# A FNet and SwiGLU block on one core: five of the second products by Strassen's seven products in place of eight

## The chip, the core and the metric

The kernel runs on one core of a Trainium2 chip. The engines named below are PE (TensorE, the matmuls), DVE (VectorE), ACT (ScalarE), POOL (GpSimd, which here issues the adding DMAs) and SP (SyncE, which issues the other DMAs). The metric is the device time of one execution in microseconds (us); a shorter time is better.

## The reference

An adaptive layer norm and a Fourier mixing layer come first (sequence 2048, width 512), then a second adaptive layer norm gives `h`, and then the gated feed-forward block, which is where the change is:

```python
gate = jnp.einsum("bsd,df->bsf", x, w1)      # 2048 x 512 times 512 x 1792
up   = jnp.einsum("bsd,df->bsf", x, w3)
h    = _silu(gate) * up                      # 2048 x 1792
out  = jnp.einsum("bsf,fd->bsd", h, w2)      # 2048 x 1792 times 1792 x 512
...
x = x + gb * out                             # gb: one factor for each of the 512 columns
```

All data are float32.

## The kernel before

**Tiles.** Everything is held transposed: 128 features on the partitions, 512 sequence positions (one of four chunks t = 0 to 3) in the free dimension. The 1792 inner features are cut into seven groups g of 256. The chunks are worked on in pairs: the first pair is chunks 0 and 2, the second pair chunks 1 and 3. A step i of the last loop is one group of one pair: steps 0 to 4 are groups 2 to 6 of the first pair, steps 5 to 11 are groups 0 to 6 of the second pair.

**Precision.** A float32 product is made of three matmuls (`PASSES`, line 42): each operand is split into a rounded high part and the low rest, and high x high, high x low and low x high are added in one PSUM bank. The high part is a copy by ACT (`copy`, L87), the low part a subtraction by DVE (`minus`, L90). So every operand that TensorE multiplies costs one instruction on ACT and one on DVE.

**Units.** TensorE's work in this part comes in units of six matmuls of 128x512. The first products of a step (with w1, called a, and with w3, called b) are already done by the Strassen-Winograd scheme in seven units a1 to a7 and b1 to b7 (`factor`, from line 1239), in which several units add into one PSUM bank after another, with a read of the bank by ACT or DVE between. The second products of a step (with w2, called y) are eight plain units, one for each chunk of the pair and each 128 output columns (`down_unit`, line 1115): two halves of the group, three matmuls each. ACT reads the bank, scales it by gb (`copy_by`, L335) into half of a tile `y`, and after every second unit POOL issues a DMA that adds the tile onto `sums` in device memory (L1146). The last two groups of the second pair don't use `sums`: DVE adds their products onto `xr`, which `load_sums` has read back (L1106), and SP stores it.

**Order.** A written list sets the order of the units: `body` and `head` near line 1660 hold, for each step, its own units, the last three b units of the step before ("-b7 -b4 -b3"), and a "y" wherever the next unit of the second products of the step before is taken from the queue `seconds`. Everything else hangs on the units. `behind(n, fn)` holds a piece of ACT or DVE work back by n units. `jobs` is a queue of the splitting of the weights (and their Strassen sums): after each unit `beside` lets as many of them go as a budget of DVE and ACT time for that unit allows; `drain` makes those that a unit needs go at once. Tiles come from a pool of 50 slots, first freed first taken, so a tile may have to wait for whatever last read its slot, an adding DMA too. All engines run their own instructions in order.

Of the kernel before, what the change touches and what calls it, by code (L numbers as in the profile page):

```python
# [8 lines left out]
F32 = mybir.dt.float32  # L9
# [6 lines left out]
P = 128  # L16
# [26 lines left out]
def folded(nc, pools, c, cp, wmr, wmc, x, xt, ctr, cti, wdr, wdi, w1, w3, w2, out):  # L43
# [22 lines left out]
    def give(t):  # L66
        slot, _ = slot_of.pop(id(t))
        free.append(slot)
# [26 lines left out]
    def times(dst, a, b):  # L95
        nc.vector.tensor_tensor(out=dst, in0=a, in1=b, op=OP.mult)  # L96
# [1018 lines left out]
    def down_unit(g, pair, t, d, key):  # L1115
        last = g == NG - 1

        own = pair == 1 and g >= NG - 2
        if not own and d % 2 == 0:
            ys[0] = take(F32, "y")  # L1120

        parts = 2 if own and last and (t, d) == (NT - 1, ND - 1) else 1
        for n in range(parts):
            at = slice(n * N // parts, (n + 1) * N // parts)
            to = bank(down_banks[0] + turn[1] % down_banks[1])[:, at]
            turn[1] += 1
            for q in range(2):
                product(
                    to,
                    [u[:, q, cols(d)] for u in wuse[key]],  # L1130
                    [hf[g, t, q][:, b, at] for b in range(2)],
                    q == 0,
                    q == 1,
                )
            if own:
                xs = xr[t][d // 2][:, d % 2, at]
                nc.vector.scalar_tensor_tensor(
                    xs, to, gb[:, d : d + 1], xs, op0=OP.mult, op1=OP.add
                )
                if last:  # L1140
                    nc.sync.dma_start(out[t, d, :, at], xs)
            else:
                copy_by(ys[0][:, d % 2, :], to, gb[:, d : d + 1])
        if not own and d % 2 == 1:
            y = ys.pop(0)
            nc.gpsimd.dma_start(sums[t, d // 2], y, accum_op=OP.add)  # L1146
            behind(4, lambda: give(y))
            if last:
                behind(8, lambda i=d // 2: store(t, i))
        if d == ND - 1:  # L1150
            for q in range(2):
# [56 lines left out]
    TO = {1: 0, 6: 0, 7: 0, 4: 0, 2: 1, 5: 2, 3: 2}  # L1208
    state, vs = {}, {}

    def right(pair, n):
        t0, t1 = PAIRS[pair]
        if n in (1, 2, 3):
            at = {1: (t0, 0), 2: (t0, 1), 3: (t1, 1)}[n]
            return h2h[at], h2l[at]
        at = pair, {5: 1, 6: 2, 7: 3, 4: 4}[n]
        return th[at], tl[at]

    def result(i, w, q, k, src):

        g, pair = items[i]
        v = vs[i][q][:, k, :]
        if w == "w1":
            behind(k != 0 or q == 0, lambda: nc.scalar.activation(v, src, AF.Silu))  # L1224
            return
        times(v, v, src)

        def highs():
# [8 lines left out]
        behind(2, lows)  # L1237

    def factor(i, w, n):
# [18 lines left out]
        if n == 1:  # L1258
            st["x"] = take(F32, "x")
            if w == "w1":  # L1260
                vs[i] = [take(F32, "v") for _ in range(2)]
        if n == 5:
            st["y"] = take(F32, "x")
        if n in (1, 5, 6):
            copy(st["y" if n == 5 else "x"][:, n // 6, :], to)
        elif n == 4:
            result(i, w, 1, 0, to)
        else:

            own = st["y" if n == 7 else "x"][:, n % 2 if n < 7 else 0, :]  # L1270
            q, k = {2: (0, 0), 3: (0, 1), 7: (1, 1)}[n]
            dst = vs[i][q][:, k, :] if w == "w1" else own
            plus(dst, to, own)
            result(i, w, q, k, dst)
            if n == 7:
                behind(1, lambda: give(st["y"]))
        if n == 3:
            for x in wuse.pop(key).values():
                give(x)
            behind(1, lambda: give(st["x"]))  # L1280
            if w == "w3":
                for x in vs.pop(i):
                    behind(3, lambda x=x: give(x))


    loads.extend((n, m) for n in range(len(steps)) for m in range(2))
# [289 lines left out]
                up_block(g, t, q, w)  # L1576
                beside(2.72, USED[w])

    def down(g, pair, t, d, key):
        drain(lambda: (key, "l") in done, jobs)  # L1580
        delayed()
        down_unit(g, pair, t, d, key)
        beside(1.36, USED["own" if pair == 1 and g >= NG - 2 else "y"])

    for w in ("w1", "w3"):
# [25 lines left out]
    def other_operands():  # L1611
# [6 lines left out]
                give(h.pop((0, n)))  # L1618
        sum_parts(jobs, *sums_of.pop())

    def unit(kind, i, n):
# [12 lines left out]
        if (kind, n) == ("a", 1) and more:  # L1634
            load_w(("w1", *items[i + 1]))
        if (kind, n) == ("a", 6):
            load_w(("w2", g, pair))
        if (kind, n) == ("a", 3) and more:
            load_w(("w3", *items[i + 1]))
            weight_jobs(i + 1, "w1")  # L1640
        if (kind, n) == ("b", 2):
            plain_jobs(("w2", g, pair))
        if (kind, n) == ("b", 3):
            if i + 2 == turning:
                drain(lambda: ("xc", 3) in done)
# [5 lines left out]
            if more:  # L1651
                weight_jobs(i + 1, "w3")
            for t in PAIRS[pair]:
                seconds.extend((g, pair, t, d, ("w2", g, pair)) for d in range(ND))
        beside(1.36, FACTOR[kind][n])

    weight_jobs(0, "w3")
# [1 line left out]
    ln2(3)  # L1659
    for i in range(len(items)):  # L1660
        body = "a6 a5 y a7 y y a4 y a3 y b1 y b2 y b6 b5 y"
        if i == turning:
            body = "y y y y y a6 y a5 y a7 y b1 b2 a4 b6 a3 b5"
        if i == len(items) - 1:
            body = "a6 a5 y a7 y y a4 y a3 b1 y b2 b6 b5 y b7 y b4 y b3 y y y y y y y y"
        head = "-b7 a1 -b4 -b3 a2 " if i == turning else "-b7 a1 a2 -b4 -b3 " if i else "a1 a2 "
        for at in (head + body).split():
            if at == "y":
                if (i, len(seconds)) == (len(items) - 1, 4):
                    tc.mark_branch_hint_location("general", hint="LikelyTaken")  # L1670
# [809 lines left out]
```

## Time and profile before

| | |
|---|---|
| median of three runs | 711.03 us (710.54 to 712.84) |
| the profiled execution | 708.46 us, its span 706.7 us |
| PE busy | 686.3 us, 97% of the span |
| DVE busy | 548.3 us, 78% |
| ACT busy | 430.8 us, 61% |
| POOL busy | 119.4 us, 17% |
| chain that ended last | PE 81%, DVE 7%, ACT 6% |

The chain is followed back from the last instruction: at each step to what released it, or to the instruction before it on its engine. A matmul's row in the trace is longer (0.39 us) than the distance to the next one, because matmuls overlap; the distance is what counts. The steps 6 to 11, which the change touches, run from about 501 us to the end.

### The profile page before, as it was taken

Reading aid. Unit: us, or ns where it says so; the run is one execution under the profiler, and the core shown is the slowest. Engines: PE = TensorE matmul, PEld = TensorE weight load, DVE = VectorE, ACT = ScalarE, POOL = GpSimd, SP = SyncE. Lnnn points to the kernel's source line nnn. Section 1 sums busy time; section 2 is a strip of 40 time slices with the busy share of each in tenths; the row PEclk is TensorE's granted clock in tenths of the full one; section 3 lists DMA queues with packets and bytes.
Section 4 is the critical chain, followed back from the end, with each engine's and each line's share of the span. In section 5 each row is a group of like instructions: output and inputs, shape, how many; then the busy total and the mean of one; then the engine's idle time right before and its main releaser. Section 6 shows DMA issues by size and latency. Waiting matters only on the chain.

```text
span 706.7 us, 8912 instructions
## 1 busy us (share of the span) xinstructions
PE 686.3 (97%) x3152; PEld 564.7 (80%) x3152; DVE 548.3 (78%) x877; ACT 430.8 (61%) x709; POOL 119.4 (17%) x141
## 2 busy tenths in 40 slices
PE   7999999999999999899999999999999999999995
PEld 4898888888888888687888788787788888888784
DVE  5999679997999978579987886896865556664763
ACT  4998865545454655745677676867665565656420
POOL 1320253542524000200100101011010100101000
PEclk9999999999999999999999999999999999999998
DMA  8730299796678521522868558376763847537403
GB/s 266 211 120 1 77 373 328 251 307 229 207 283 287 168 86 41 92 58 64 209 114 199 89 130 153 61 156 137 239 136 73 180 62 175 111 69 162 137 0 124
DMA packets 38100, 108.93 MB, mean 154 GB/s; under 512 B 4896, under 2 KB 5152, under 8 KB 38048
## 3 DMA queue, kind: packets, MB, share of 16 engines
q0 software_dynamic: 12352, 43.00, 29.3%
q1 hardware_dynamic: 25264, 63.98, 27.5%
q10 hardware_dynamic: 432, 1.31, 0.5%
q8 instruction: 26, 0.43, 0.3%
q14 instruction: 26, 0.21, 0.1%
HBM read 76.81 MB, written 33.55 MB: 156 GB/s over the span
## 4 chain that ended last, share of the span: by engine, by line
PE 81%; DVE 7%; ACT 6%; issue 2%; DMA 2%; SPq 1%; ACTq 0%; DVEq 0%
PE bank L100 52%; PE bank L750 25%; PE bank L559 2%; PE bank L598 1%; DMA wmr<-in_wmr 1%; ACT xc L894 1%; PE bank L576 1%; DVE xc L96 1%; SPq L231 1%; ACT hf L87 1%; ACT y L335 1%; DVE v L96 0%; DVE hl L90 0%; ACT hm L501 0%; DMA w<-in_wdi 0%
## 5 line engine op out<-in xcount | busy, mean ns | idle before, releaser
L100 PE MATMUL bank<-hf,w2h 128*128 128x512 f32 (+1 forms) x452 | 140.9, 391 | 0.3
L1146 POOL DMA_DIRECT2D sum<-y x48 | 41.0, 855 | 390.1 <-ACT y L335 373.0
L100 PEld LDWEIGHTS bank<-hf,w2h 128*128 128x128 f32 x452 | 84.3, 188 | 22.1 <-DVE hf L90 3.4
L100 PE MATMUL bank<-hf,w2l 128*128 128x512 f32 (+1 forms) x226 | 87.6, 388 | 0.0
L87 ACT ACTIVATE hf<-v 128x512 fp32r<-128x512 f32 x56 | 35.3, 630 | 67.3 <-DVE v L96 62.7
L335 ACT ACTIVATE y<-bank,gb 128x512 f32<-128x512 f32 x96 | 64.9, 682 | 18.6 <-PE bank L100 18.3
L93 DVE TENSOR_TENSOR v<-bank,x 128x512 f32<-128x512 f32 x36 | 24.7, 685 | 34.9 <-PE bank L100 34.8
L750 PE MATMUL bank<-bh,us 128*128 128x512 f32 x128 | 49.9, 390 | 0.0
L93 DVE TENSOR_TENSOR x<-bank,x 128x512 f32<-128x512 f32 x36 | 24.7, 687 | 32.4 <-PE bank L100 28.7
L750 PE MATMUL bank<-bh,ul 128*128 128x512 f32 x128 | 49.8, 389 | 0.0
L750 PE MATMUL bank<-d,us 128*128 128x512 f32 x128 | 49.8, 389 | 0.0
L750 PE MATMUL bank<-d,uh 128*128 128x512 f32 x128 | 49.8, 389 | 0.0
L750 PE MATMUL bank<-l,us 128*128 128x512 f32 x128 | 49.8, 389 | 0.0
L750 PE MATMUL bank<-l,uh 128*128 128x512 f32 x128 | 49.8, 389 | 0.0
L100 PEld LDWEIGHTS bank<-hf,w2l 128*128 128x128 f32 x226 | 42.4, 188 | 8.4
L90 DVE TENSOR_TENSOR hf<-v,hf 128x512 fp32r<-128x512 f32 x56 | 38.5, 687 | 12.2 <-ACT hf L87 12.1
L170 POOL DMA_INDIRECT re<-in_ctr,mirror x32 | 35.8, 1117 | 66.2 <-DVE ul L90 39.5
L1224 ACT ACTIVATE v<-v 128x512 f32<-128x512 f32 x36 | 22.8, 632 | 38.8 <-DVE v L93 38.8
L87 ACT ACTIVATE x<-bank 128x512 f32<-128x512 f32 x72 | 41.4, 586 | 7.2 <-PE bank L100 6.5
L170 POOL DMA_INDIRECT im<-in_cti,mirror x32 | 32.7, 1023 | 35.3 <-PE bank L750 10.0
L100 PE MATMUL bank<-h2h,w1h 128*128 128x512 f32 x80 | 31.8, 397 | 1.5 <-ACT h2h L87 1.5
L100 PE MATMUL bank<-h2l,w1h 128*128 128x512 f32 x80 | 31.9, 399 | 0.8 <-DVE h2l L90 0.8
(246 smaller groups left out, 1775.2 us busy)
## 6 DMA issues: line engine op xcount, KB each, us to landing
sum<-y POOLq DMA_DIRECT2D x48, 512.0 KB, 5.6
w<-in_w SPq DMA_DIRECT2D x42, 512.0 KB, 4.5
re<-in_ctr SPq DMA_DIRECT2D x32, 256.0 KB, 5.0
im<-in_cti SPq DMA_DIRECT2D x32, 256.0 KB, 5.0
wmc<-in_wmc SPq DMA_DIRECT2D x8, 512.0 KB, 6.3
xr<-in_xt SPq DMA_DIRECT2D x8, 512.0 KB, 7.6
sum<-xr SPq DMA_DIRECT2D x8, 512.0 KB, 6.2
x<-in_x SPq DMA_DIRECT2D x11, 256.0 KB, 4.8
```

What stands on the lines that cost most here:

```text
L87: nc.scalar.activation(dst, src, AF.Copy, scale=scale)
L90: nc.vector.tensor_tensor(out=dst, in0=a, in1=b, op=OP.subtract)
L93: nc.vector.tensor_tensor(out=dst, in0=a, in1=b, op=OP.add)
L96: nc.vector.tensor_tensor(out=dst, in0=a, in1=b, op=OP.mult)
L100: nc.tensor.matmul(acc, lhs[a], rhs[b], start=first and n == 0, stop=last and n == len(PASSES) - 1, skip_group_check=more,)
L170: nc.gpsimd.indirect_dma_start(dst, None, rows, bass.IndirectOffsetOnAxis(ap=at, axis=0))
L231: queue.dma_start(raw_w[dt][q * 64 : (q + 1) * 64, m, :], w[i][par::2, q])
L335: nc.scalar.activation(dst, src, AF.Identity, scale=by)
L559: nc.tensor.matmul(halves(hb[k])[:, m, :], sides((hh, hl)[a][k])[:, dt, m, :], wu[dt][:, b, m, :], start=False, stop=dt % 2 == 1 and n == ...
L750: nc.tensor.matmul(acc[what, e], lhs, rhs, start=begin and i == 0, stop=(end or (turn and what == "x")) and i == len(terms) - 1, skip_grou ...
L1146: nc.gpsimd.dma_start(sums[t, d // 2], y, accum_op=OP.add)
L1224: behind(k != 0 or q == 0, lambda: nc.scalar.activation(v, src, AF.Silu))
```

## The change

For groups 0 to 4 of the second pair (steps 5 to 9) the second products are done by seven products instead of eight units. A product of this kind is also six matmuls: three into bank 6 and three into bank 7, for one chunk-sized right operand. Three of the seven start new sums in the two banks and four add onto what is there, and after each of them ACT copies both banks, scaled by gb, to a tile y that POOL adds onto `sums`. The right operands are four quarters of the gated product and three sums of them; the weights w2 get sums and a split of the sums, as w1 and w3 have. The order of the units is written anew for steps 6 to 11, with a seven-product unit after every two units of first products. The splitting of w3 for the next step is queued earlier (after b6 instead of after b3), and in step 5 that of w1 after a7 instead of a3. `load_sums` of both chunks now follows the seventh product of group 4, in step 11.

```diff
+    SEVEN = [(g, 1) for g in range(NG - 2)]
+    ORDER7 = (2, 5, 3, 1, 6, 7, 4)
+    LEFT7 = {1: "h0", 2: "h2", 4: "h3", 5: "s0", 6: "s1", 7: "s2", 3: "s3"}
+    TO7 = {2: (0, 0), 5: (1, 1), 3: (0, 1), 1: (0, 0), 6: (0, 1), 7: (1, 1), 4: (1, 0)}
...
+    def seven_parts(i, q, k):
...
+        if (q, k) != (0, 1):
+            n = {(0, 0): 1, (1, 0): 2, (1, 1): 3}[q, k]
+            behind(1, lambda: high(n, v[q, k]))
+            behind(2, lambda: low(n, v[q, k]))
+            return
+        t1, t2, t3, t4 = v[0, 0], v[1, 1], v[0, 1], v[1, 0]
+        behind(1, lambda: minus(t1, v[0, 1], v[0, 0]))
+        behind(2, lambda: high(5, t1))
+        behind(2, lambda: minus(t3, v[1, 1], v[0, 1]))
+        behind(3, lambda: low(5, t1))
+        behind(3, lambda: minus(t2, v[1, 1], t1))
+        behind(4, lambda: high(7, t3))
+        behind(4, lambda: minus(t4, v[1, 0], t2))
+        behind(5, lambda: high(6, t2))
+        behind(5, lambda: low(7, t3))
+        behind(6, lambda: high(4, t4))
+        behind(7, lambda: low(6, t2))
+        behind(8, lambda: low(4, t4))
+
+    def seven_jobs(key):
...
+        step(jobs, 1, highs, 0.0, 1.0)
+        step(jobs, 1, totals, 1.4)
+        step(jobs, 1, lows, 1.2)
+        step(jobs, 1, sum_highs, 0.0, 1.0)
+        step(jobs, 1, sum_lows, 1.2)
+
+    def seven_unit(g, pair, n, key):
+        new = n in (1, 2, 5)
+        if new:
+            banks7[:] = [bank(6), bank(7)]
+        y = take(F32, "y")
...
+        for e, to in enumerate(banks7):
+            at = int(LEFT7[n][1]) * HALF + e * P
+            product(
+                to,
+                [flat(wuse[key][x])[:, at : at + P] for x in names],
+                [u[:, b, :] for b in range(2)],
+                new,
+                True,
+                not new,
+            )
+            d = 2 * which + e
+            copy_by(y[:, e, :], to, gb[:, d : d + 1])
+        give(u)
+        nc.gpsimd.dma_start(sums[t, which], y, accum_op=OP.add)
+        behind(4, lambda: give(y))
+        if n == ORDER7[-1]:
...
+            if g == NG - 3:
+                for t in PAIRS[pair]:
+                    load_sums(t)
...
-        if (kind, n) == ("a", 3) and more:
+        if (kind, n) == ("a", 7 if i == turning else 3) and more:
             load_w(("w3", *items[i + 1]))
             weight_jobs(i + 1, "w1")
         if (kind, n) == ("b", 2):
-            plain_jobs(("w2", g, pair))
+            (seven_jobs if (g, pair) in SEVEN else plain_jobs)(("w2", g, pair))
...
+        if (kind, n) == ("b", 6) and more and early_w3(i):
+            weight_jobs(i + 1, "w3")
...
         body = "a6 a5 y a7 y y a4 y a3 y b1 y b2 y b6 b5 y"
+        if i and items[i - 1] in SEVEN:
+            body = "a6 a5 a7 y a4 a3 y b1 b2 y b6 b5 y"
+        spread = i > 1 and items[i - 2] in SEVEN
+        if spread and i < len(items) - 1:
+            body = body.replace("a6", "a6 y", 1)
...
         if i == len(items) - 1:
-            body = "a6 a5 y a7 y y a4 y a3 b1 y b2 b6 b5 y b7 y b4 y b3 y y y y y y y y"
+            body = "a6 a5 a7 a4 a3 b1 b2 y b6 y b5 y b7 y b4 y y b3 y y y y y y y y y y"
         head = "-b7 a1 -b4 -b3 a2 " if i == turning else "-b7 a1 a2 -b4 -b3 " if i else "a1 a2 "
+        if spread and i < len(items) - 1:
+            head = "-b7 a1 y a2 -b4 y -b3 "
+        if i == len(items) - 1:
+            head = "-b7 y a1 a2 y -b4 -b3 y "
```

The order of the instructions on the engines, at two places.

**A steady step.** ACT's queue over the end of step 7 and the head of step 8 (the tiles `x` are bank reads of the first products, `hf` high parts of right operands, `w2sh`, `w3h`, `w3sh` high parts of weights and their sums). Before, from the high part of w3 on:

```order
L87 ACTIVATE w3h_5323<-w_817_5180 128x1024
L87 ACTIVATE hf_5331<-v_5055 128x512
L87 ACTIVATE x_5290<-bank_838_5283 128x512
L87 ACTIVATE w3sh_5344<-w3s_5325 128x1024
L87 ACTIVATE x_5354<-bank_851_5347 128x512
L335 ACTIVATE y_5358<-bank_855_5359,gb 128x512
L1224 ACTIVATE v_5292<-v_5292 128x512
L335 ACTIVATE y_5358<-bank_856_5375,gb 128x512
```

In the changed kernel, from the high part of the sums of w2 on; y_5322 is read from the two banks of product 1, y_5365 from those of product 6, which adds onto the same banks:

```order
L87 ACTIVATE w2sh_5305<-w2s_5290 128x1024
L87 ACTIVATE x_5314<-bank_852_5307 128x512
L87 ACTIVATE w3h_5318<-w_834_5229 128x1024
L335 ACTIVATE y_5322<-bank_856_5320,gb 128x512
L335 ACTIVATE y_5322<-bank_857_5321,gb 128x512
L87 ACTIVATE hf_5345<-v_5094 128x512
L87 ACTIVATE x_5354<-bank_861_5347 128x512
L87 ACTIVATE w3sh_5362<-w3s_5332 128x1024
L335 ACTIVATE y_5365<-bank_856_5320,gb 128x512
L335 ACTIVATE y_5365<-bank_857_5321,gb 128x512
```

The reads of y come in pairs, and each pair now stands behind a wide copy of weights that stood elsewhere before.

**The last step.** DVE's queue in step 11, from the low part of the sums of w3 on (`v` with a bank is a first product's read by DVE, `xr` the adding of a plain second product). Before:

```order
L90 TENSOR_TENSOR w3sl_5834<-w3s_5803,w3sh_5822 128x1024
L1137 SCALAR_TENSOR_TENSOR xr_5645<-bank_943_5836,gb,xr_5645 128x512
L93 TENSOR_TENSOR v_5772<-bank_928_5763,x_5832 128x512
L1137 SCALAR_TENSOR_TENSOR xr_5645<-bank_944_5852,gb,xr_5645 128x512
L1137 SCALAR_TENSOR_TENSOR xr_5646<-bank_945_5860,gb,xr_5646 128x512
L1137 SCALAR_TENSOR_TENSOR xr_5646<-bank_946_5875,gb,xr_5646 128x512
L93 TENSOR_TENSOR v_5771<-bank_940_5825,x_5770 128x512
L1137 SCALAR_TENSOR_TENSOR xr_5749<-bank_949_5900,gb,xr_5749 128x512
L93 TENSOR_TENSOR x_5898<-bank_950_5908,x_5898 128x512
L96 TENSOR_TENSOR v_5771<-v_5771,x_5898 128x512
L90 TENSOR_TENSOR w2l_5919<-w_937_5818,w2h_5917 128x1024
```

In the changed kernel:

```order
L90 TENSOR_TENSOR w3sl_5955<-w3s_5915,w3sh_5943 128x1024
L93 TENSOR_TENSOR v_5875<-bank_957_5866,x_5964 128x512
L93 TENSOR_TENSOR v_5874<-bank_976_5957,x_5873 128x512
L93 TENSOR_TENSOR x_5996<-bank_980_5998,x_5996 128x512
L96 TENSOR_TENSOR v_5874<-v_5874,x_5996 128x512
L90 TENSOR_TENSOR w2l_6009<-w_974_5953,w2h_6007 128x1024
L1137 SCALAR_TENSOR_TENSOR xr_5933<-bank_984_6013,gb,xr_5933 128x512
L90 TENSOR_TENSOR hf_6011<-v_5874,hf_6011 128x512
```

The low part of the last w2 (w2l) came after five of the xr adds and now comes before the first of them, and the read of a7's bank (v_5875<-bank_957) stands right behind the low part of the sums of w3, with no second product between a7 and a4.

## Rows read from the trace of the kernel before

**Rows 1.** First part of the page: busy us (share of the span) xinstructions.
```profile
PE 686.3 (97%) x3152; PEld 564.7 (80%) x3152; DVE 548.3 (78%) x877; ACT 430.8 (61%) x709; POOL 119.4 (17%) x141
```

**Rows 2.** Busy time by stretch: two steps (engines' us and counts, clock, DMA share, GB/s).
```profile
511.00:541.20 30.20, 30.20 (x134) 24.73 (x133) 17.89 (x29) 18.26 (x28) 3.40 (x4) 1.00 0.60 122
541.20:571.40 30.20, 30.20 (x133) 24.72 (x133) 17.88 (x28) 18.28 (x28) 3.40 (x4) 1.00 0.59 122
```

**Rows 3.** Timeline of PE at a second product: start us, us, instruction.
```profile
572.33 0.84 PE L100 MATMUL bank<-hf,w2h 128*128 128x512 f32 x2
573.01 0.40 PE L100 MATMUL bank<-hf,w2l 128*128 128x512 f32 x1
573.25 0.39 PE L100 MATMUL bank<-th,w1sh 128*128 128x512 f32 x1
...
577.34 0.39 PE L100 MATMUL bank<-th,w1h 128*128 128x512 f32 x1
```

**Rows 4.** Waits of PE's weight loads, 511 to 632 us: total, times, longest.
```profile
PEld bank L100 <- DVE hf L90: 1.5, 4, 0.4
```

**Rows 5.** Timeline of POOL: two adding DMAs four steps apart.
```profile
533.15 0.85 POOL L1146 DMA_DIRECT2D sum<-y  x1 [5.95 <-ACT y L335]
...
653.82 0.85 POOL L1146 DMA_DIRECT2D sum<-y  x1 [5.95 <-ACT y L335]
```

**Rows 6.** Timeline of PE at the start of step 6.
```profile
503.44 0.50 PE L100 MATMUL bank<-h2h,w1l 128*128 128x512 f32 x1 [0.21 <-DVE w1l L90]
```

**Rows 7.** Timeline of DVE, steps 5 and 6.
```profile
492.00 0.69 DVE L93 TENSOR_TENSOR v<-bank,x 128x512 f32<-128x512 f32 x1 [3.97 <-PE bank L100]
...
510.13 0.42 DVE L93 TENSOR_TENSOR w3s<-w 128x256 f32<-128x256 f32 x1
...
511.60 0.68 DVE L90 TENSOR_TENSOR hf<-v,hf 128x512 fp32r<-128x512 f32 x1
512.21 1.22 DVE L90 TENSOR_TENSOR w3l<-w,w3h 128x1024 fp32r<-128x1024 f32 x1
513.34 0.68 DVE L90 TENSOR_TENSOR hf<-v,hf 128x512 fp32r<-128x512 f32 x1
```

**Rows 8.** Timeline of ACT, step 11.
```profile
648.98 0.64 ACT L87 ACTIVATE hf<-v 128x512 fp32r<-128x512 f32 x1 [1.30 <-DVE v L96]
649.51 0.67 ACT L335 ACTIVATE y<-bank,gb 128x512 f32<-128x512 f32 x1
650.11 0.60 ACT L87 ACTIVATE x<-bank 128x512 f32<-128x512 f32 x1
...
662.60 1.06 ACT L87 ACTIVATE w3sh<-w3s 128x1024 fp32r<-128x1024 f32 x1 [0.35 <-ACT x L87]
663.57 0.58 ACT L87 ACTIVATE x<-bank 128x512 f32<-128x512 f32 x1
...
674.33 1.05 ACT L87 ACTIVATE w2h<-w 128x1024 fp32r<-128x1024 f32 x1
```

**Rows 9.** DMA queues and issues, 541.2 to 571.4 us (issues: median us to landing).
```profile
q0 software_dynamic: 576, 2.10, 44.7%
q1 hardware_dynamic: 432, 1.57, 14.5%
...
sum<-y POOLq DMA_DIRECT2D x4, 512.0 KB, 6.5
w<-in_w SPq DMA_DIRECT2D x3, 512.0 KB, 5.9
```

**Rows 10.** The same, 601.6 to 631.8 us.
```profile
sum<-y POOLq DMA_DIRECT2D x4, 512.0 KB, 5.3
```

**Rows 11.** Timeline of SP's queue, step 11.
```profile
652.56 7.38 SPq L1106 DMA_DIRECT2D xr<-sum  x2
660.04 0.38 SPq L1035 DMA_DIRECT2D w<-in_w  x1
```

**Rows 12.** Busy time by stretch, around the longest waits of PE in this part.
```profile
296.00:298.00 2.00, 0.53 (x2) 0.22 (x2) 1.23 (x1) 2.00 (x3) 0.28 (x1) 0.88 1.13 207
298.00:300.00 2.00, 2.00 (x5) 1.61 (x6) 1.52 (x2) 1.46 (x2) 1.03 (x2) 0.50 1.01 201
```

More of the change, by code (lines that the diff above doesn't have):

```diff
@@ L1209, in folded @@
     state, vs = {}, {}
+    SEVEN = [(g, 1) for g in range(NG - 2)]
+    ORDER7 = (2, 5, 3, 1, 6, 7, 4)
+    LEFT7 = {1: "h0", 2: "h2", 4: "h3", 5: "s0", 6: "s1", 7: "s2", 3: "s3"}
+    TO7 = {2: (0, 0), 5: (1, 1), 3: (0, 1), 1: (0, 0), 6: (0, 1), 7: (1, 1), 4: (1, 0)}
+    right7, banks7 = {}, []
     def right(pair, n):
@@ L1226, in result @@
         times(v, v, src)
+        if (g, pair) in SEVEN:
+            seven_parts(i, q, k)
+            return
         def highs():
@@ L1237, in result, with high, low @@
         behind(2, lows)
+    def seven_parts(i, q, k):
+        key = items[i]
+        v = {(a, b): vs[i][a][:, b, :] for a in range(2) for b in range(2)}
+        def high(n, src):
+            right7[key, n] = take(F32R, "hf")
+            copy(right7[key, n][:, 0, :], src)
+        def low(n, src):
+            u = right7[key, n]
+            minus(u[:, 1, :], src, u[:, 0, :].bitcast(F32))
+        if (q, k) != (0, 1):
+            n = {(0, 0): 1, (1, 0): 2, (1, 1): 3}[q, k]
+            behind(1, lambda: high(n, v[q, k]))
+            behind(2, lambda: low(n, v[q, k]))
+            return
+        t1, t2, t3, t4 = v[0, 0], v[1, 1], v[0, 1], v[1, 0]
[11 more added lines that the diff above has]
+        behind(8, lambda: low(4, t4))
@@ new lines, in seven_jobs, with highs, totals, lows @@
+    def seven_jobs(key):
+        use = wuse[key] = {}
+        def highs():
+            use["h"] = take(F32R, "w2h")
+            copy(flat(use["h"]), flat(wraw[key]))
+        def totals():
+            use["s"] = take(F32, "w2s")
+            s, r = four(use["s"]), four(wraw[key])
+            plus(s[:, 0, :], r[:, 1, :], r[:, 3, :])
+            minus(s[:, 1, :], s[:, 0, :], r[:, 0, :])
+            minus(s[:, 2, :], r[:, 0, :], r[:, 1, :])
+            minus(s[:, 3, :], r[:, 2, :], s[:, 1, :])
+        def lows():
+            use["l"] = take(F32R, "w2l")
+            r = wraw.pop(key)
+            minus(flat(use["l"]), flat(r), flat(use["h"]).bitcast(F32))
+            give(r)
+        def sum_highs():
+            use["sh"] = take(F32R, "w2sh")
+            copy(flat(use["sh"]), flat(use["s"]))
+        def sum_lows():
+            use["sl"] = take(F32R, "w2sl")
+            minus(flat(use["sl"]), flat(use["s"]), flat(use["sh"]).bitcast(F32))
+            give(use.pop("s"))
+            done.add((key, "l"))
+        step(jobs, 1, highs, 0.0, 1.0)
[3 more added lines that the diff above has]
+        step(jobs, 1, sum_lows, 1.2)
@@ new lines, in seven_unit @@
+    def seven_unit(g, pair, n, key):
[3 more added lines that the diff above has]
+        y = take(F32, "y")
+        which, k = TO7[n]
+        t = PAIRS[pair][k]
+        names = ("h", "l") if LEFT7[n][0] == "h" else ("sh", "sl")
+        u = right7.pop(((g, pair), n))
+        for e, to in enumerate(banks7):
[14 more added lines that the diff above has]
+        if n == ORDER7[-1]:
+            for x in wuse.pop(key).values():
+                give(x)
+            if g == NG - 3:
+                for t in PAIRS[pair]:
+                    load_sums(t)
@@ L1282, in factor @@
                 for x in vs.pop(i):
-                    behind(3, lambda x=x: give(x))
+                    behind(9 if items[i] in SEVEN else 3, lambda x=x: give(x))
     loads.extend((n, m) for n in range(len(steps)) for m in range(2))
@@ L1577, in up, with down @@
                 beside(2.72, USED[w])
-    def down(g, pair, t, d, key):
+    def down(g, pair, *which):
+        key = which[-1]
         drain(lambda: (key, "l") in done, jobs)
         delayed()
-        down_unit(g, pair, t, d, key)
+        if (g, pair) in SEVEN:
+            seven_unit(g, pair, *which)
+        else:
+            down_unit(g, pair, *which)
         beside(1.36, USED["own" if pair == 1 and g >= NG - 2 else "y"])
@@ L1619, in other_operands, with early_w3 @@
         sum_parts(jobs, *sums_of.pop())
+    def early_w3(i):
+        return items[i] in SEVEN
     def unit(kind, i, n):
@@ L1650, in unit @@
                 other_operands()
-            if more:
+            if more and not early_w3(i):
                 weight_jobs(i + 1, "w3")
-            for t in PAIRS[pair]:
-                seconds.extend((g, pair, t, d, ("w2", g, pair)) for d in range(ND))
+            if (g, pair) in SEVEN:
+                seconds.extend((g, pair, n, ("w2", g, pair)) for n in ORDER7)
+            else:
+                for t in PAIRS[pair]:
+                    seconds.extend((g, pair, t, d, ("w2", g, pair)) for d in range(ND))
+        if (kind, n) == ("b", 6) and more and early_w3(i):
+            weight_jobs(i + 1, "w3")
         beside(1.36, FACTOR[kind][n])
```

## The prediction, made before the changed kernel was timed

> **What bounds the kernel now.** I read the busy shares first: PE is busy 97% of the span, DVE 78%, ACT 61% [rows 1]. Then the stretch that the change touches, cut into whole steps: PE is busy all of 30.2 us, DVE 17.9, ACT 18.3 [rows 2]. So here time goes only by what PE has to do, and the other two have 12 us to spare in a step. Then PE's timeline, for the price of a matmul: from 573.25 to 577.34 there are 18 matmuls, 0.2272 us each, so a unit of six takes 1.363 us [rows 3]. Four steps take 653.82 - 533.15 = 120.67 us by their adding DMAs, 30.17 each [rows 5], where 22 units would take 29.99. The 0.18 left over is one wait: two matmuls that should take 0.45 take 0.68 (572.33 to 573.01) [rows 3], because a weight load waits for the low part of a gated product, 0.38 each time, four times in four steps [rows 4].
>
> **The change part by part.** The profiled execution took 708.46 us, 2.57 below the median of 711.03; I add up against the first and move the median by the sum.
>
> Matmuls. Five groups lose a unit each: 5 x 6 = 30 matmuls, 30 x 0.2272 = 6.8 us, all on PE's path.
>
> Waits that go. The second products no longer begin right behind the low parts of the gated product, so the wait of 0.2 us should go in the five steps: 1.0 us. At 503.44 PE waited 0.21 us for the low part of w1 [rows 6]; in step 5 the w1 pieces are now queued after a7, five units earlier, and DVE sits idle then (3.97 us before 492.00 [rows 7]): 0.2 us. Together 8.0 us. Both ends: 6.8 if other waits of that size come instead, 8.0.
>
> Work added per group, at the distance between one instruction and the next. DVE: four sums of weights 511.60 - 510.13 = 1.47 us, one low part of 1024 columns 513.34 - 512.21 = 1.13, four subtractions and three low parts of 512 columns at 512.21 - 511.60 = 0.61 [rows 7]: 6.9 us. ACT: six more reads into y at 0.60, three high parts at 0.53, one wide copy at 0.97 [rows 8]: 6.2 us. A step shrinks to 21 x 1.363 = 28.6 us, so DVE is busy 17.9 + 6.9 = 24.8 (87%) and ACT 18.3 + 6.2 = 24.5 (86%). PE's work covers both sums. What is not covered is a place where PE needs one certain instruction and it stands behind others in its queue. I looked for those places.
>
> Step 6. From its read at 492.00 [rows 7] (the last a unit of step 5) to its read of step 6's a7, DVE's new queue holds 17 instructions of 512 columns (10.4 us), three sets of weight sums (4.4) and six low parts of 1024 (6.8): 21.6 us, done at 513.6. PE starts step 6's second unit about 502.6 (three matmul distances and the wait before 503.44 [rows 6]), so a7, the eighth, ends at 502.6 + 7 x 1.363 = 512.1. Its bank can be read from 512.3, and a4, which adds onto it, is due one unit later at 513.5. DVE reads from 513.6 to 514.3. PE loses 0.85 us. Before there were two units between a7 and a4.
>
> Steps 7 to 10. I walked ACT's queue from b2 on, with zero at the start of b7 of step 7 and 1.363 a unit. DVE begins a3's read at 19.3 and has four instructions of 512 columns, the sums of w1 and two low parts of 1024 (6.2 us) up to the gated product of b2, so ACT's high part behind that goes at 25.6. Product 3's two reads, b6's read, w2sh, b5's read, w3h and product 1's two reads follow without a gap: 3 x 0.53 + 4 x 0.60 + 2 x 0.97 = 5.9. Product 1's reads end at 31.0 and 31.5; product 6 adds onto bank 6 from 31.4 and onto bank 7 from 32.0. The next high part waits for DVE, which comes to b7's gated product at 32.7 (sums of w2 and w3 stand before it); behind it are a1's read, w3sh and product 6's reads, of which the first ends at 32.7 + 2 x 0.53 + 0.97 + 0.60 = 35.3, and product 7 wants the bank at 35.4. So the spacing of two units is just enough, with 0.1 to 0.5 us in hand. I take a loss of 0.3 us a step, 1.2 in all; the ends are 0 and one unit (1.36) a step, 5.5.
>
> Step 11, with zero at the start of b7 of step 10. Three losses. First, product 4's reads wait in ACT's queue behind a high part (b3's product is there at 10.9); they end at 12.8, w3sh takes until 13.7, a6's read until 14.3. a7 adds onto that bank and is due at 13.7: 0.65 us. Second, DVE behind b3: weight sums, two low parts of 512 columns, two of 1024, so w3sl ends at 15.9; a7's bank is read until 16.6, but a4 now follows a7 directly and is due at 15.7: 0.9 us. Third, SP. `load_sums` now follows product 4: xr_5934 must wait for its adding DMA, 12.8 + 0.3 + 5.3 (landing when little else runs [rows 10]) = 18.4 us. Behind it stand two more xr loads and the last w2, as the w2 load stood 7.4 us behind xr loads before [rows 11]. Four transfers of 512 KB at 14.5% x 30.2 / 3 = 1.46 us each [rows 9], and some 2 us until the first lands: w2 is there near 26. Before, it was issued at 660.04 [rows 11] and used at 674.33 [rows 8], 14 us later; now ACT stands before it from about 21. It is copied until 27.1, w2l until 28.2, and only then DVE reads the first plain second product, until 29.0. The third of them needs that bank at 27.6: 1.4 us, or 0 if w2 lands at 24.5, 3 if at 27.5. Sum 2.95; ends 0.5 and 6, the upper one with a lost clock: after PE had idled about 2.3 us around 296, the granted clock was 0.50 (1.2 GHz) from 298 to 300 [rows 12], which cost about 1.2 us.
>
> DMAs. 15 more adding DMAs, three more per step. POOL has the time (0.85 us each [rows 5]), and no transfer is waited for by PE; a tile y takes the slot of the one two products earlier, whose DMA lands about 6.5 us after its start [rows 9], about when it is needed. Taken at nothing; the other end is a rival below.
>
> Sum: -8.0 + 0.85 + 1.2 + 2.95 = -3.0 us. 711.03 - 3.0 = 708.0.
>
> **Weighing a rule.** Four adding DMAs held the 16 DMA engines 44.7% of 30.2 us [rows 9], 3.37 us each. Seven of them and three weight loads make 7 x 3.37 + 3 x 1.46 = 28.0 us of a step of 28.6. The Trainium skill (DMA: Bandwidth & Descriptors, "Anatomy of one DMA — SWDGE (gpsimd) path") gives a fixed 2.0 us and bytes / 436e3 us for such a DMA; by it, as an estimate, 512 KB move in 1.2 us and land in 3.2, and seven would fill 8.4 us of the step, so that the slow rival would have no chance. The trace differs: 5.3 to 6.5 us to landing [rows 9, 10]. The measurement decides, and the rival keeps its chance.
>
> **The rivals.**
> (a) The covers hold: nothing is lost in steps 6 to 10 and under 1.5 us in step 11. For it: my slacks are mostly not negative, and the budget in `beside` delays weight work. Against: step 11's two places follow from the written order. 711.03 - 8.0 + 1.5 = 704.5.
> (b) ACT and DVE pace the steps. Both are at 86 to 87% in an order with waits in both directions; if each of the four steady steps loses most of a unit, 4.5 in place of 1.2, the sum is 0.3: 711.3. For it: the hand-walk left 0.1 us at product 7. Against: both queues stand idle again behind a6 and can catch up.
> (c) Slower: the DMA engines become the bound. The adding DMAs and loads fill 28.0 of 28.6 us; if an adding DMA takes longer when the next follows after 4.1 us, y tiles wait for their slots, ACT waits with them, and PE for ACT. A step then takes 7 x X + 4.4 us; beyond X = 3.68 it is slower than the 30.17 of before. At X = 4.1 a step is 33.1, and four steps cost 11.7 us instead of winning 6.2: 711.03 + 11.7 - 1.8 (the rest of the 8.0) + 3.8 (steps 6 and 11) = 724.7, at X = 3.75 about 715. For it: landing went from 5.3 to 6.5 with weight loads beside [rows 9, 10]. Against: the share counts packets in flight, and it passes 1 where queues overlap (1.13 [rows 12]), so it is no hard limit.
>
> **How the numbers follow.** Forecast 0.50 (706.3 to 710), (a) 0.22, (b) 0.16, (c) 0.12. The range for 8 in 10 leaves out the best of (a) and all but the start of (c): 703.5 to 712.5; the forecast's own is 706.3 to 710. A measurement of this kernel tells 0.3%, 2.1 us, from no change. Faster, under 708.9: 0.36 of the forecast, all of (a), a little of (b): 0.59. Same: the rest of the forecast, most of (b): 0.27. Slower: (c) and the end of (b): 0.14.
>
> **What would show it.** In the profile after: the adding DMAs of a target in steps 7 to 10 recur every 28.6 us (29 with my losses); PE waits for DVE before a4 of step 6, for ACT before a7 and for DVE before a4 and before the third plain product of step 11; no waits of weight loads on the low parts. The forecast is wrong if steady steps take over 29.5 us (with PE waiting for ACT reads of y: (b); with ACT waiting for adding DMAs, landing over 8 us: (c)), or if step 11 shows no wait.

## The result: a little slower, with new waits of TensorE in steps 6 to 11

The changed kernel took 712.06 us (median of 22 runs, 708.07 to 715.60) against 710.20 for the kernel before (708.27 to 712.84): ratio 1.0024, 95% interval 1.0013 to 1.0036. Forecast was 708.0. The profiled execution took 711.43 us, its span is 709.6.

The first part of the page, beside [rows 1]: 30 matmul records fewer and 4.8 us less PE, 35 us more DVE and 24 us more ACT.

```profile
PE 681.5 (96%) x3122; PEld 558.7 (79%) x3122; DVE 583.3 (82%) x937; ACT 455.2 (64%) x759; POOL 131.9 (19%) x156
```

Two steps by windows, from one adding DMA of product 6 to the next (columns as in [rows 2]), then these DMAs in POOL's timeline. A step takes 29.2 to 29.5 us where it took 30.17 [rows 5]; DVE and ACT are as busy as forecast (24.8 of 24.8, 23.2 of 24.5), and PE is idle 0.16 and 0.36 us.

```profile
538.35:567.50 29.15, 28.99 (x128) 23.50 (x127) 24.82 (x40) 23.19 (x37) 5.97 (x8) 1.00 0.91 181
567.50:597.02 29.52, 29.16 (x128) 23.49 (x127) 24.81 (x40) 23.17 (x37) 5.96 (x7) 1.00 0.88 173
```

```profile
538.35 0.86 POOL L1338 DMA_DIRECT2D sum<-y  x1 [3.88 <-ACT y L335]
...
567.50 0.85 POOL L1338 DMA_DIRECT2D sum<-y  x1 [3.87 <-ACT y L335]
```

All of PE's waits from 504 us to the end, by releaser (total, times, longest). The waits for the gated product's low parts [rows 4] are gone. Those that came are the ones forecast, and at the places forecast: `v` in front of a4, `y` in front of product 7, `x` in front of a7, `xr` in front of the third plain second product. One was not forecast: one of the three before a4 is in step 8.

```profile
PE bank L100 <- DVE v L93: 2.1, 3, 1.0
PE bank L100 <- DVE xr L1137: 2.0, 1, 2.0
PE bank L100 <- ACT y L335: 0.8, 4, 0.3
PE bank L100 <- ACT x L87: 0.7, 1, 0.7
```

Their price isn't the idle time in the brackets. PE's timeline at a4 of step 6, at step 11's a7 and a4, and at the third plain product:

```profile
516.05 0.39 PE L100 MATMUL bank<-hf,w2l 128*128 128x512 f32 x1
517.48 0.50 PE L100 MATMUL bank<-th,w1h 128*128 128x512 f32 x1 [1.04 <-DVE v L93]
517.82 0.40 PE L100 MATMUL bank<-tl,w1h 128*128 128x512 f32 x1
...
661.71 0.50 PE L100 MATMUL bank<-th,w1sh 128*128 128x512 f32 x1 [0.68 <-ACT x L87]
...
664.22 0.50 PE L100 MATMUL bank<-th,w1h 128*128 128x512 f32 x1 [0.85 <-DVE v L93]
...
675.00 0.39 PE L100 MATMUL bank<-th,w3sl 128*128 128x512 f32 x1
677.39 0.74 PE L100 MATMUL bank<-hf,w2h 128*128 128x512 f32 x2 [2.01 <-DVE xr L1137]
```

From 516.05 to 517.48 are 1.43 us where 0.23 do without a wait, and the next distance is 0.34 in place of 0.23: the wait shown as 1.04 costs 1.31. I therefore add up what each distance between starts has over 0.2268 us (shorter distances are left out), and call it the loss. From the start of step 6 to the end it is 2.37 us before and 8.73 after: 4.2 in steps 6 to 10, 4.4 in step 11 and 0.2 at the end. With 30 matmuls gone (6.8 us), this part of the program runs only 0.3 us faster (203.93 us from the last plain adding DMA ahead of step 6 to the start of PE's last matmul, before 204.19), where 3.0 was forecast. The measured 1.9 us on the other side had to be looked for: in how this loss differs between executions, and in what lies ahead of step 6, where this profile is 2.8 us late (the last plain adding DMA starts at 497.07 us, before at 494.28).

### The profile page after: what moved, and what is told of

Same layout as the page of the kernel before. It is cut to its first block, busy times and chain, and to the rows that moved or that the text cites. A ratio compares the mean times of both kernels' runs of the same rounds, so it can differ in the third digit from the quotient of the medians.

```text
span 709.6 us, 9004 instructions
## 1 busy us (share of the span) xinstructions
PE 681.5 (96%) x3122; PEld 558.7 (79%) x3122; DVE 583.3 (82%) x937; ACT 455.2 (64%) x759; POOL 131.9 (19%) x156
## 3 DMA queue, kind: packets, MB, share of 16 engines
q10 hardware_dynamic: 432, 1.31, 0.5%
## 4 chain that ended last, share of the span: by engine, by line
PE 40%; issue 37%; DMA 9%; ACT 4%; POOL 4%; DVE 4%; another core or an unknown queue 1%; POOLq 0%; SPq 0%; ACTq 0%; DVEq 0%
PE bank L750 24%; PE bank L100 12%; DMA sum<-y 5%; POOL sum L1146 3%; PE bank L559 2%; POOL sum L1338 1%; DMA x<-in_x 1%; DMA w<-in_wdr 1%; PE bank L598 1%; DMA w<-in_w 1%; ACT y L335 1%; DMA w<-in_wdi 1%; PE bank L576 1%; DVE ul L90 1%
## 5 line engine op out<-in xcount | busy, mean ns | idle before, releaser
L100 PE MATMUL bank<-hf,w2h 128*128 128x512 f32 (+1 forms) x352 | 108.8, 390 | 2.4 <-DVE xr L1137 2.0
L335 ACT ACTIVATE y<-bank,gb 128x512 f32<-128x512 f32 x126 | 81.5, 681 | 8.0 <-PE bank L100 7.6
L87 ACT ACTIVATE hf<-v 128x512 fp32r<-128x512 f32 x71 | 44.3, 629 | 65.4 <-DVE v L96 53.2
L100 PEld LDWEIGHTS bank<-hf,w2h 128*128 128x128 f32 x352 | 65.5, 188 | 18.6 <-DVE xr L1137 2.8
L1146 POOL DMA_DIRECT2D sum<-y x28 | 24.0, 857 | 247.8 <-ACT y L335 234.8
L100 PE MATMUL bank<-hf,w2l 128*128 128x512 f32 (+1 forms) x176 | 68.1, 387 | 0.0
L90 DVE TENSOR_TENSOR hf<-v,hf 128x512 fp32r<-128x512 f32 x71 | 48.5, 687 | 12.5 <-ACT hf L87 12.3
L1338 POOL DMA_DIRECT2D sum<-y x35 | 29.8, 852 | 133.6 <-ACT y L335 118.0
L93 DVE TENSOR_TENSOR v<-bank,x 128x512 f32<-128x512 f32 x36 | 24.7, 687 | 23.2 <-PE bank L100 20.4
L100 PEld LDWEIGHTS bank<-hf,w2l 128*128 128x128 f32 x176 | 33.1, 188 | 6.7
```

The source lines that it names most:

```text
L87: nc.scalar.activation(dst, src, AF.Copy, scale=scale)
L90: nc.vector.tensor_tensor(out=dst, in0=a, in1=b, op=OP.subtract)
L93: nc.vector.tensor_tensor(out=dst, in0=a, in1=b, op=OP.add)
L100: nc.tensor.matmul(acc, lhs[a], rhs[b], start=first and n == 0, stop=last and n == len(PASSES) - 1, skip_group_check=more,)
L335: nc.scalar.activation(dst, src, AF.Identity, scale=by)
L1338: nc.gpsimd.dma_start(sums[t, which], y, accum_op=OP.add)
```

## Experiments

The theory, **W**: PE pays for its waits in steps 6 to 11 one by one, so each can be taken away alone and the savings add up. Rivals: queues so full that a wait only moves (**queues**); reloads or adding DMAs as the late ones; and something outside these steps that comes with the longer program (**P**). Each group of runs has its own runs of before, so ratios are compared.

**The changed kernel again** (no edit).


> The changed kernel, unedited. Theory W (waits): what the change costs lies in steps 6 to 11 alone: PE's waits there sum to 8.7 us against 2.4 of before, 30 matmuls go (6.8 us), so the two kernels should come out within 0.5 us of each other in a profile in which the part before step 6 runs alike; then the last plain adding DMA before step 6 starts near 494.3 us as before, and the 2.8 us by which it was late in the first profile (0.8 in the first 25 us, 2.0 at 87 to 92 us, where VectorE stood 4.2 us before a read) were chance. Theory P (program): the program is longer, something is fetched later, and the 2.8 us before step 6 come back in every profile of it: VectorE stands about 4 us near 87 us again and the adding DMA starts near 497. Time by W 709.7 to 710.5, by P 712 or more, with before at 710.2.


Measured 712.15 us, ratio 1.0030 (1.0011 to 1.0049): the time is P's, not W's. The loss from step 6 on was 8.50 us, and this part ran 0.4 us faster than before. Ahead of it VectorE's stand at 87 to 91 us was there again (it idles some 4 us before one read of a bank; PE lost 1.8), but the 0.8 us of the first 25 us was not, and the last plain adding DMA started at 495.78 us, between what the two theories gave. So far P fits for the stand.

**w2 asked for before the reloads.**
```
-        if (kind, n) == ("a", 6):
+        if (kind, n) == ("a", 6 if more else 1):
             load_w(("w2", g, pair))
```


> One edit to the changed kernel: in the last step the last load of w2 is asked for behind a1, ahead of the four reloads of the sums, in place of behind a6, after them. Theory W: the wait of 2.16 us before the third plain second product goes (and nothing takes its place, since w2h, w2l and w3's work stand ready): 2.2 us less than the unedited change, 1.5 to 2.5. Rival (reloads): the reloads of the sums themselves come too late, since they wait for product 4's adding DMA; then the same place waits for xr and gains under 0.7 us.


Measured 709.50 us, ratio 0.9987 (0.9976 to 0.9998): 3.0 us less than the unedited kernel by the ratios, and the `xr` wait is gone. SP asks for w2 at 643.05 us, 12 us ahead of the reloads, and ACT copies it without a wait:

```profile
643.05 0.33 SPq L1035 DMA_DIRECT2D w<-in_w  x1
655.19 12.79 SPq L1106 DMA_DIRECT2D xr<-sum  x4
```

```profile
669.91 1.05 ACT L87 ACTIVATE w2h<-w 128x1024 fp32r<-128x1024 f32 x1
```

W holds for this wait; the rival (reloads) falls. The gain is above the 1.5 to 2.5 us expected from the first profile; a later run shows why.

**a3 ahead of a4.**
```
-            body = "a6 a5 a7 y a4 a3 y b1 b2 y b6 b5 y"
+            body = "a6 a5 a7 y a3 a4 y b1 b2 y b6 b5 y"
...
-            body = "a6 a5 a7 a4 a3 b1 b2 y b6 y b5 y ...
+            body = "a6 a5 b1 a7 a3 b2 a4 y b6 y b5 y ...
```
(in these steps the pieces of w1 are given back after a4).


> One edit to the changed kernel: in steps 6 to 10 a3 runs ahead of a4, so that two units lie between a7 and a4, and the last step runs a6 a5 b1 a7 a3 b2 a4 in place of a6 a5 a7 a4 a3 b1 b2. Theory W: the waits before a4 go (1.3 us in step 6, about 0.5 in step 8) and both waits in step 11 before a7 and a4 (0.95 and 1.12): 3.0 to 3.9 us less than the unedited change. Rival (queues): VectorE is 86% busy, so the read that PE waited for is only late by what stands ahead of it, and the next unit in need of VectorE (a3, which now comes earlier, or b2) waits in its place: under 1.5 us.


Measured 711.07 us, ratio 1.0006 (0.9990 to 1.0023). By the time alone neither is met: the ratios give 1.7 us less than the unedited kernel, where W gave 3.0 to 3.9 and the rival under 1.5. The trace tells more. All waits before a4, a7 and product 7 are gone; two small ones are new. But `xr` has grown from 2.0 to 5.5:

```profile
PE bank L100 <- DVE xr L1137: 5.5, 1, 5.5
PE bank L100 <- ACT y L335: 0.6, 1, 0.6
PE bank L100 <- DVE w3l L90: 0.2, 1, 0.2
```

Counted from the last plain adding DMA ahead of step 6, PE came to the third plain product 5.2 us sooner than in the unedited profile beside it, and SP to the request for w2 only 2.0: product 4's adding DMA was issued 3.6 us sooner, but the reload behind it left SP 7.3 us after that, where 5.7 passed in the unedited profile. So the time that the order gained went into a longer wait for w2. I hadn't expected the waits before product 7 to go: with a3 a unit earlier the copy `w3sh`, which had stood ahead of product 6's reads in ACT's queue, ran before the high part there.

**The plan's budget.**
```
-        beside(1.36, USED["own" if pair == 1 and g >= NG - 2 else "y"])
+        used = USED["own" if pair == 1 and g >= NG - 2 else "y"]
+        beside(1.36, (0.0, 1.2) if (g, pair) in SEVEN else used)
```


> One edit to the changed kernel: the plan that places weight work beside a unit counts 1.2 us of ScalarE for each of the seven products (their two reads) in place of 0.6 us, so weight copies are put later in ScalarE's queue. Theory W: the reads of product 6 wait behind w3's copy of sums (0.97 us) in ScalarE's queue; the waits before product 7 (0.43 us, four times) go or halve: 0.8 to 1.8 us less than the unedited change. Rival (adding DMAs): the reads are late because y tiles wait for their adding DMAs; then the waits stay, under 0.4 us. Third possibility: the weights come late instead and PE waits for w1 or w3: slower.


The edit moved no instruction on any engine, so it tested nothing of the kind, and counts as one more profile of the unedited program: ratio 1.0066 (1.0042 to 1.0090), the same waits before product 7 (0.7 us in four), and an `xr` wait of 2.1 with PE's granted clock at 0.50 behind it.

**Both edits** (the two diffs above together).


> The two edits that helped, together: the last w2 load ahead of the reloads of the sums, and a3 ahead of a4 in steps 6 to 10 with a6 a5 b1 a7 a3 b2 a4 in the last step. Theory W (PE pays for its waits in steps 6 to 11 one by one, and they add up): with the order alone 1.3 us of waits are left in these steps beside the 5.7 us wait for the last w2 and about 2 us at the halved clock behind it; with w2 there in time both of these go, so PE loses 1.3 us against 8.7 in the changed kernel: 7 us under it, 704 to 705.5, ratio to before 0.992 to 0.994, and runs closer together, since no wait is long enough for the clock to be halved. Rival (reloads): in the new order PE comes to the plain second products 5 us sooner, and the reloads of the sums, which wait for product 4's adding DMA, are now the late ones: a wait of 2 to 4 us at the first plain second products, ratio 0.997 to 1.0.


Measured 701.09 us, ratio 0.9903 (0.9884 to 0.9922): 6.9 us faster than before. Waits from step 6 on, then two steps by windows; the loss from step 6 on is 1.8 us.

```profile
PE bank L100 <- ACT y L335: 0.5, 1, 0.5
PE bank L100 <- DVE w3l L90: 0.2, 1, 0.2
```

```profile
533.43:561.74 28.31, 28.31 (x126) 23.42 (x126) 24.59 (x40) 23.35 (x38) 5.97 (x8) 1.00 0.91 186
561.74:590.30 28.56, 28.56 (x128) 23.66 (x127) 24.79 (x40) 23.28 (x38) 5.96 (x8) 1.00 0.88 176
```

W predicted 704 to 705.5 where before takes 710 to 711, and the ratio came out below its 0.992 to 0.994. By the ratios the two edits alone gave 3.0 and 1.7 us, together 9.0, so the savings did not simply add up as W has it: what the order saves shows only where the wait for w2 doesn't take it up. The steady step is the 28.6 us of 21 units, with PE never idle, DVE at 87%, and the same seven adding DMAs. So in this order neither the queues nor the DMA engines bound it.

**Before, a second profile, and before with longer programs that run nothing more.**
```
+    spare = take()                       # in the branch that is not run
+    nc.vector.memset(flat(spare), 0.0)
+    for _ in range(59):
+        nc.vector.tensor_tensor(...)
+    for _ in range(50):
+        nc.scalar.activation(...)
```


> The kernel before, unedited, for a second profile of the part ahead of step 6. Five profiles of the changed kernel and its variants all show VectorE standing 3.5 to 4.3 us before one read of a bank at 87 to 91 us, and PE 0.9 to 1.6 us behind it; the one profile of before shows 1.73 us there and no wait of PE. Theory P (it belongs to the changed program): no such stand here. Rival (chance): the stand is here too, with PE's wait of 0.9 to 1.6 us.

> The kernel before with 60 more VectorE and 50 more ScalarE instructions (what the change adds) in the branch that is not run, so that the two engines' programs are longer and not a single instruction more is executed. Theory P1 (the length of the programs moves where instructions lie and when they are fetched): VectorE's stand at 87 to 91 us appears here, PE loses 0.9 to 1.6 us at that place, and the time goes up by that: ratio 1.001 to 1.0025. Rival: no stand, ratio 1.000 within 0.001; then it is not the mere length of the programs.


No stand in either; the longer one measured 707.50 us, ratio 0.9996 (0.9985 to 1.0007). Mere length, at least this way, costs nothing. In the second profile of before PE was 2.8 us behind the first one after 20 us, and its last plain adding DMA ahead of step 6 started at 496.38 us (494.28 in the first), so the part ahead of step 6 varies by itself.

**The changed kernel and before once more, side by side.**


> The changed kernel, unedited, beside the kernel before on the same chip, each with a profile. VectorE's stand at 87 to 91 us was in the first five profiles of the changed kernel and its variants, and in none of the last three (two of before, one of a variant). Theory P (it comes with the changed program): the stand is here and not in the profile of before that follows. Rival S (it comes with the chip or the hour): both profiles show it or neither does. Time: the wait for the last w2 before the third plain second product, 1.6 to 2.3 us in the profiles, with a halved clock behind it in one of three, should again make this kernel 1 to 2 us slower than before: ratio 1.001 to 1.003; without the stand 1.000 to 1.002.

> The kernel before, unedited, for its profile on the same chip as the changed kernel. Theory P: VectorE waits 1.7 us before its read at 88 to 91 us, for the bank, and PE nothing there. Rival S: the same as in the changed kernel's profile beside it.


The unedited kernel measured 713.74 us, ratio 1.0058 (1.0040 to 1.0077), above what I expected. Its profile shows why. PE's timeline at the third plain product, the windows around it (columns as in [rows 2]), and the chain of waits in front:

```profile
674.23 0.39 PE L100 MATMUL bank<-th,w3sl 128*128 128x512 f32 x1
678.72 1.04 PE L100 MATMUL bank<-hf,w2h 128*128 128x512 f32 x2 [4.10 <-DVE xr L1137]
679.55 0.63 PE L100 MATMUL bank<-hf,w2l 128*128 128x512 f32 x1
```

```profile
674.00:678.00 4.00, 0.61 (x3) 0.19 (x1) 1.23 (x2) 2.31 (x4) 0.00 (x0) 1.00 0.05 17
679.00:682.00 3.00, 3.00 (x8) 2.31 (x8) 1.42 (x3) 0.00 (x0) 0.00 (x0) 0.50 0.03 5
682.50:685.00 2.50, 2.50 (x12) 2.04 (x11) 1.52 (x3) 0.11 (x1) 0.00 (x0) 1.00 0.00 0
```

```profile
667.86 0.35 SPq L1106
...
668.30 7.36 DMA w<-in_w
...
675.69 1.06 ACT w2h L87
...
677.92 0.76 DVE xr L1137
678.67 0.04 issue
678.72 6.47 PE bank L100 x20
```

The same wait as in the first profile, but 4.26 us by the distance of starts, and behind it some 3 us at a granted clock of 0.50 (1.2 GHz): 6.0 us at this one place, 13.2 from step 6 on. In the first profile the same load was asked for at 668.25 and took 6.09 us in the chain; here it was asked for at 668.30 and took 7.36, while PE stood at the product 0.8 us sooner. The request came no sooner because product 4's adding DMA, issued 0.8 us sooner, held the reload behind it for 7.2 us in place of 6.4 (rows below). The lost clock isn't of this profile alone: the mean granted clock of the six executions is 0.989 to 0.991, that of before in the same group 0.994 by the median.

The stand of VectorE was in the unedited kernel's profile (PE lost 1.75 us) and this time in that of before as well (1.1):

```profile
90.28 0.69 DVE L93 TENSOR_TENSOR ho<-bank,ho 128x512 f32<-128x512 f32 x1 [3.60 <-remote]
```

So the changed program isn't alone in having it, against P, and before lost less by it, against the rival.

**w2 early, a3 ahead of a4 in steps 6 to 10 only** (the last step's order as in the changed kernel).
```
-            body = "a6 a5 a7 y a4 a3 y b1 b2 y b6 b5 y"
+            body = "a6 a5 a7 y a3 a4 y b1 b2 y b6 b5 y"
...
-        if (kind, n) == ("a", 6):
+        if (kind, n) == ("a", 6 if more else 1):
```


> The changed kernel with two edits: the last w2 load ahead of the reloads of the sums, and a3 ahead of a4 in steps 6 to 10; the last step's order is that of the changed kernel. Theory W: against the version with all edits only step 11's two waits come back, 0.95 before a7 and 1.12 before a4: 2.1 us more than that version, ratio to before 0.9925 to 0.9945 (that version: 0.990). Rival (room): steps 6 to 10 finish 4 us sooner, so that in step 11 the work ahead of these two reads is no longer late, and the two waits are gone without the last step's order: ratio 0.990 to 0.992.


Measured 704.35 us, ratio 0.9925 (0.9906 to 0.9945), at the lower edge of what W gave. The two waits of step 11 stand where they stood (2.1 us of loss with what follows), so the rival (room) falls by the trace, though not by the ratio's interval alone:

```profile
PE bank L100 <- DVE v L93: 0.9, 1, 0.9
PE bank L100 <- ACT x L87: 0.7, 1, 0.7
```

**The account.** Loss from step 6 on in the profile; this part against before, read from the trace (from the last plain adding DMA ahead of step 6 to the start of PE's last matmul; before takes 204.19 us); loss at the stand at 90 us; and the measured difference, which is the ratio's distance from 1 times the median of before in its group.

| kernel | loss | this part | stand | measured |
|---|---|---|---|---|
| changed, first profile | 8.73 | -0.3 | 1.7 | +1.7 |
| changed, again | 8.50 | -0.4 | 1.8 | +2.1 |
| changed (budget edit) | 10.15 | +1.2 | 1.7 | +4.7 |
| changed, third | 13.24 | +4.4 | 1.75 | +4.1 |
| w2 early | 7.14 | -1.8 | 1.85 | -0.9 |
| a3 ahead of a4 | 9.46 | +0.3 | 1.0 | +0.4 |
| w2 early, a3 in steps 6 to 10 | 3.41 | -5.8 | 1.8 | -5.3 |
| all edits | 1.81 | -7.4 | 0 | -6.9 |

A profile is one execution and the measured column comes from many, so single rows may differ by some us. From the ratios the steps are: w2 early 3.0 us (against the second row, in the same group), a3 ahead of a4 in steps 6 to 10 4.4, the last step's order 1.6. The last two compare different groups; four sets of runs of the unedited program alone gave ratios from 1.0024 to 1.0066, so they are rough. Behind PE's last matmul the changed program and its variants take 8.3 to 8.8 us in the profiles, before 7.8 to 8.2; no term of the forecast has this difference, and I haven't traced it.

## Why the prediction was wrong

The new waits stood where the prediction put them; their sizes failed, in two terms of the sum. Steps 6 to 10 were to cost 0.85 + 1.2 = 2.05 us: they lost 4.2 in the first profile and 3.9 to 5.0 in four others of the same order, and a3 ahead of a4 gave back 3.7 between the profiles and 4.4 by the ratios. The wait for the late w2 was put at 1.4 us: it lost between 1.7 and 6.0 in four profiles of the unedited program, and asking for w2 earlier gave back 3.0. The adding DMAs, taken at nothing, have a part in both. Term by term:

- **Matmuls, 6.8 us: right.** A step of 21 units in place of 22 is 28.6 us, and with all edits it takes just that.
- **Waits that go, 1.2 us: too small.** 2.2 us went. I took the bracket's 0.2 at the low part of w1 where the distances lose 0.48, counted five of six low-part waits of 0.23 [rows 3], and left out 0.34 us in step 11.
- **Step 6, 0.85 us: right in place and cause, 1.31 in size.** DVE's read of a7 begins at 516.74, 0.35 us later than walked (513.6, with this profile 2.8 us late); another 0.11 is the distance behind the wait.
- **Steps 7 to 10, 1.2 us: 2.4 (2.2 to 3.3 in the other profiles), and 0.4 more in step 6 in front of product 1.** The place forecast, product 7 behind product 6's reads, has 0.43 to 0.55 us each time. ACT's queue is as walked, the wait for DVE, a read, `w3sh`, then the two reads; where I had 0.1 us in hand, 0.2 to 0.3 are missing:

```profile
534.84 0.63 ACT L87 ACTIVATE hf<-v 128x512 fp32r<-128x512 f32 x1 [1.50 <-DVE v L96]
535.38 0.58 ACT L87 ACTIVATE x<-bank 128x512 f32<-128x512 f32 x1
535.85 1.05 ACT L87 ACTIVATE w3sh<-w3s 128x1024 fp32r<-128x1024 f32 x1
536.80 1.26 ACT L335 ACTIVATE y<-bank,gb 128x512 f32<-128x512 f32 x2
```

 Besides it a4 waits in step 8 (0.47), which I had not walked; its cause is under DMAs below.
- **Step 11, 2.95 us with 1.4 for the late w2: too small.** The two waits ahead of it cost 0.95 and 1.12 (forecast 0.65 and 0.9). The `xr` wait lost 2.3 us in the first profile; in later ones of the same instructions 1.7, 4.0 (1.6 of it at the halved clock) and 6.0. The mechanism is as forecast: SP asks for w2 only after four reloads, of which the second waits for product 4's adding DMA, and ACT, DVE and PE each stand behind the copy. From that reload to the copy of w2 7.5 us pass, walked 7.6 (18.4 to 26). What I had too short is the landing of the adding DMA: 5.3 us, from a stretch before with four such DMAs in 30 us [rows 10]. Product 4's adding DMA, the reload behind it and the request for w2, in the first profile and then in the third:

```profile
660.52 0.85 POOL L1338 DMA_DIRECT2D sum<-y  x1 [3.89 <-DVE hf L90]
666.88 1.27 SPq L1106 DMA_DIRECT2D xr<-sum  x3
668.25 0.38 SPq L1035 DMA_DIRECT2D w<-in_w  x1
```

```profile
659.71 0.86 POOL L1338 DMA_DIRECT2D sum<-y  x1 [3.89 <-DVE hf L90]
666.94 1.27 SPq L1106 DMA_DIRECT2D xr<-sum  x3
668.30 0.38 SPq L1035 DMA_DIRECT2D w<-in_w  x1
```

 From the DMA's issue to the reload are 6.4 and 7.2 us; in the two other profiles of these instructions 5.7 and 6.5. The load of w2 itself took 6.1 us in three of the four and 7.4 in the third. I gave each of these a single value, and I had named the lost clock and put it at the far end of the range (6 us in all) instead of giving it weight: the forecast wait was 1.4 us, and one of 2.25 already had the lower clock behind it.
- **DMAs, nothing: nearly right.** The rival of DMA engines as the bound is refuted: they are 88 to 91% busy in steps of 28.3 to 28.6 us when all edits are in, with PE never idle. The Trainium skill's formula (DMA: Bandwidth & Descriptors, "Anatomy of one DMA — SWDGE (gpsimd) path") would land an adding DMA of 512 KB in an estimated 3.2 us; the trace with all edits shows medians of 5.7 and 6.6 in these two steps, with seven to a step, where four to a step had 5.3 to 6.5 [rows 9, 10]. But the sentence that no transfer is waited for by PE is wrong. In step 8 of the first profile the adding DMA issued at 567.50 took 7.72 us in the chain (6.5 assumed); ACT's read of a5's bank waits for it, as its tile x takes a slot that the DMA still reads; DVE's read of a7 needs that x; and a4 waits for DVE, 0.47 us of loss:

```profile
567.50 7.72 DMA sum<-y
```

```profile
575.33 0.60 ACT L87 ACTIVATE x<-bank 128x512 f32<-128x512 f32 x1 [1.45 <-DMA sum<-y]
575.96 0.69 DVE L93 TENSOR_TENSOR v<-bank,x 128x512 f32<-128x512 f32 x1 [1.18 <-ACT x L87]
576.70 0.50 PE L100 MATMUL bank<-th,w1h 128*128 128x512 f32 x1 [0.20 <-DVE v L93]
```

 In the third profile the same chain cost 0.58 and 0.54 us in two steps (ACT waited 1.58 and 1.54 there). Where ACT waited 1.13 us or less for the DMA, PE lost 0.11 or nothing. No run takes this wait away by itself.
- **The rivals.** The time fell near that of (b), 711.3, and in part by its cause: the steady steps wait for ACT and DVE, but lost 2.2 to 3.3 us over four steps, between my 1.2 and the 4.5 of (b). One of three steady steps took 29.52 us, just over the 29.5 that was to speak for (b), the others 29.15 and 29.05. The rest of the loss came from step 11 and from outside these steps, so that the time is so near is chance. (a), 704.5 with the covers holding, is what the kernel does once the two orders are put right (701.1 where before takes 708.0).
- **What stays open.** VectorE's stand near 90 us, in seven of eight profiles with the change and one of four without. Its instructions and their order are the same there in both programs, and the trace names no releaser that I could follow. If these shares hold, it is about 1 us of the measured difference. Length of the programs alone did not bring it. The part ahead of step 6 also varies by the clock: behind PE's two waits near 296 us the granted clock is 0.50 in five of the eight profiles with the change and in two of the four without, which moves PE by about 1.2 us in either program.

## What to carry over

When work is taken off the bounding engine, walk each queue that feeds it to the end of the program, the DMA queue too: here a load left behind transfers that wait for the last result cost the most of any single wait, and asking for it earlier cost nothing that the trace shows. A forecast for such a wait needs its spread and the clock behind it, not one value. And where an edit removes waits but the time stays, look in the trace for a later wait that grew by as much.

## What the runs showed of the hardware

- A wait costs more than its idle time in the trace: 1.31 us for 1.04, 0.95 for 0.68, 1.12 for 0.85. Of the 0.27, 0.16 is how the bracket counts (from the end of the row before, 0.39 us long, while the next matmul was due after 0.23), and 0.11 is a longer distance to the matmul behind.
- After PE had waited 2.25 us (by distance of starts), 4.26 and 5.66 in step 11, the granted clock was 0.50 for some 3 us of matmuls; after 1.62 and 2.16 at the same place it was not.
- One load of 512 KB, asked for behind three reloads, took 6.09 us in one execution and 7.36 in another, with 668.25 and 668.30 us as the times of the request. An adding DMA of 512 KB held the reload behind it for 5.7 to 7.2 us from its issue, in four profiles of the same instructions.
